# Another written order for the first eleven stretches of a layernorm, attention and gate kernel

## Chip, core and metric

The kernel runs on one core of a Trainium2 chip. The metric is device microseconds of one execution; a time given for a kernel is the median of its runs.

In the text, PE is TensorE (the matmul engine), DVE is VectorE, ACT is ScalarE, POOL is GpSimd and SP is SyncE, which here only issues transfers. PEld is the loading of weights into PE. "SPq" marks the work of SP's queue.

## What is computed

The input x has 2048 rows of 640. Its rows are normalised (mean and variance); the result xn goes through windowed attention with 32 heads of 192 against cached keys and values, whose last 512 positions alone count, and through an output projection. Beside that a small expert layer picks the two rows of xn with the largest score, passes them through a gated feed-forward layer and adds the result to these rows; a silu of that gates the attention.

```python
def _A_ref(x, k_cache, v_cache, wq, wo):
    W = min(4096, max(256, Sk // 4))
    q = (x @ wq).reshape(B, Sq, Hq, Dh) ...
    scores = einsum("bhqd,bhkd->bhqk", q, k) * (Dh ** -0.5)
    p = softmax(scores, axis=-1)
    o = einsum("bhqk,bhkd->bhqd", p, v)
    return o.transpose(...).reshape(B, Sq, Hq * Dh) @ wo

xn = _layernorm(x, axis=-1)
s = _A_ref(xn, A_k_cache, A_v_cache, A_wq, A_wo)
g = _silu(_B_ref(xn, B_w_r, B_w_gate, B_w_up, B_w_down))
return x + s * g
```

All inputs and the output are bf16; W is 512.

## The kernel before

**Tiling.** The 2048 rows are 16 tiles of 128. The 32 heads go in eight groups of four, a group in two pairs of heads. A step is one group, one block of four tiles (t5) and one pair; a unit is one tile of a step, so that unit n belongs to step n // 4 and there are 256 units. A unit's work: scores of both heads (128 x 512 each, two matmuls a head because 192 = 128 + 64), the row maximum, the exponential with its sum, a transpose of the probabilities by DMA, P V (eight matmuls), a division by the sums, a transpose of the output by DMA. Two units of the same tile in the two pairs of a group then give one output projection (W), which is added up in s_acc over the groups.

**Stretches.** The units are put into stretches: units 0 and 1, units 2 and 3, then three at a time (4 to 6, 7 to 9, and so on, line 90); unit 36 is the third of stretch 12. In a stretch the scores of its units come first, then the maxima and exponentials, while PE does query products, P V of the stretch before and output projections.

**Order.** The kernel sets the order of the instructions on every engine itself (line 46). A program text of tokens is walked, and every token appends its instructions to the engines that it uses; each engine and each engine's DMA queue works through its own instructions in that order and waits at each for its operands. The text FIRST (line 853) is written by hand for stretches 0 to 10; from stretch 11 on stretch() (line 823) makes the tokens by a rule. The tokens that matter here:

- `x.t.lo.hi` loads tiles lo to hi of block t of x, on SP's queue, with `.a` on ACT's (load_x, line 98; two blocks have room, so block 2 waits until block 0 has been normalised); `k.p.h` loads the keys of a head of pair p (line 114), `wq.p`, `v.p`, `wo.g.h` the weights and values.
- `bn.n.c` takes the statistics of half a tile on DVE, the second half adds the aggregate (line 162). `as.n` takes a whole tile's on ACT in two passes (line 230), with a small step on POOL. `sq` and `rc` make 1/sqrt of the variance for tiles 0 and 1 on ACT and DVE; `pw.lo.hi` makes it for two to four tiles in four small POOL steps (line 211). `sx` and `ex` have ACT load the Sqrt and the Exp table.
- `ap.n.e` normalises tile n into xn on engine e: `v` DVE, `a` ACT, `g` POOL (line 245).
- `turn.n.e` transposes a tile of xn on PE and copies it out of PSUM on engine e (line 257); `xT.lo.hi` does it by DMA (line 263). `kt.q.e` transposes half the first pair's keys on PE (line 267); `kT.p` does a later pair's by DMA.
- `q.i.c` is a query product: a third c of the pair's queries for all four tiles of step i, five matmuls; with `.lo.hi` for a part of the tiles (line 297). `qe.i.c.e` scales it out of PSUM into qT on engine e (line 307).
- `S.j` scores, `M.n.h` maximum of a head (DVE), `E.n.h` exponential (ACT), `P.n` transpose of the probabilities (SP's queue), `R.j` reciprocals of the sums, `O.n` P V, `Oe.n.e` its eviction with the division, `T.j` transpose of a stretch's outputs (SP's queue), `W.w` output projection, `We.w.e` its eviction.
- `z.1` is a matmul of zeros that nobody reads. `B.j.s` runs what the expert layer has due there; in stretches 0 to 10 nothing is due, so these tokens do nothing.

**PSUM.** Six buffers ("p", one bank each) rotate through scores, projections, the keys' turns and those P V outputs that are written `OO.a.b` or `O.n.g`; two buffers ("f") rotate through query products, the turns of xn and the P V outputs written `O.n` (lines 72 to 79). A buffer is free when its eviction has run.

**The token's engine letter.** first() (line 654) reads it from the last field alone:

```python
op, *n = token.split(".")
e = n[-1] if n and n[-1] in "avgh" else None
n = [int(c) for c in n if c not in "avgh"]
```

scaled() (line 290) uses DVE for "v" and ACT for anything else.

Of the kernel before, what the change touches and what calls it, by code (L numbers as in the profile page):

```python
# [21 lines left out]
def kernel(ctx, tc, A_x, A_k_cache, A_v_cache, A_wq, A_wo, B_x, B_w_r, B_w_gate, B_w_up, B_w_down, out):  # L22
    nc = tc.nc
    P = 128
    _, S, D = A_x.shape
# [88 lines left out]
    def k_load(p, hh, eng):  # L114
        if hh == 0:
            kraw_of[p] = kraw_pool.tile([P, NJ, 2, Dh], BF16, name="k_raw")
        eng.dma_start(out=kraw_of[p][:, :, hh, :], in_=k_win[2 * p + hh].rearrange("(p j) d -> p j d", j=NJ))
# [536 lines left out]
    def first(token):  # L654
        op, *n = token.split(".")
        e = n[-1] if n and n[-1] in "avgh" else None
# [255 lines left out]
```

## Time and profile before

| what | us |
|---|---|
| median of three runs | 797.73 (797.13 to 799.15) |
| profiled execution | 799.47 |
| its span, first to last instruction | 797.7 |
| PE busy | 783.4 (98%) |
| DVE busy | 623.7 (78%) |
| ACT busy | 479.8 (60%) |
| POOL busy | 175.9 (22%) |

A row of a timeline has the start, the length, the engine (ending in q for an issued transfer), the line of the kernel, the operation, what it writes and reads, and how many were merged into it; a bracket at its end has the time that the engine stood idle before it, and what ended that. The length of a merged transfer row is that of its issues on the queue's engine with the waits between. A row of a group has line, engine, operation, what it writes and reads, shapes, count, then busy us and the mean ns of one, then the idle time before them. A row of windows has the window and its length, then the busy us of each engine with its instructions, the granted clock of PE as a share of full speed, the DMA share and GB/s. Matmuls overlap, so the times of single matmul rows can run into each other by a fraction of a microsecond.

### The profile page before, as it was taken

Reading aid. Unit: us, or ns where it says so; the run is one execution under the profiler, and the core shown is the slowest. Engines: PE = TensorE matmul, PEld = TensorE weight load, DVE = VectorE, ACT = ScalarE, POOL = GpSimd, SP = SyncE. Lnnn points to the kernel's source line nnn. Section 1 sums busy time; section 2 is a strip of 40 time slices with the busy share of each in tenths; the row PEclk is TensorE's granted clock in tenths of the full one; section 3 lists DMA queues with packets and bytes.
Section 4 is the critical chain, followed back from the end, with each engine's and each line's share of the span. In section 5 each row is a group of like instructions: output and inputs, shape, how many; then the busy total and the mean of one; then the engine's idle time right before and its main releaser. Section 6 shows DMA issues by size and latency. Waiting matters only on the chain.

```text
span 797.7 us, 15636 instructions
## 1 busy us (share of the span) xinstructions
PE 783.4 (98%) x5751; PEld 482.3 (60%) x5751; DVE 623.7 (78%) x1242; ACT 479.8 (60%) x1291; POOL 175.9 (22%) x193
## 2 busy tenths in 40 slices
PE   7889999999999999999999999999999999999998
PEld 4456556665666665666656666666665666656666
DVE  6976658989787777777787777777788988777786
ACT  5976666555656555665556565556666876565652
POOL 1320000000000000000000499980000000265966
PEclk9999999999999999999999999999999999999999
DMA  8999997799979999799998899979997899997995
GB/s 236 206 213 208 187 197 133 140 183 199 179 123 218 186 209 212 134 216 210 181 215 156 168 180 205 164 121 184 196 184 131 132 186 205 177 199 145 182 165 146
DMA packets 453773, 143.80 MB, mean 180 GB/s; under 512 B 422350, under 2 KB 453328, under 8 KB 453696
## 3 DMA queue, kind: packets, MB, share of 16 engines
q1 hardware_dynamic: 450512, 139.63, 94.4%
q0 software_dynamic: 736, 1.84, 0.8%
q10 hardware_dynamic: 2448, 1.33, 0.6%
q8 instruction: 45, 0.74, 0.4%
q14 instruction: 32, 0.26, 0.1%
HBM read 39.98 MB, written 2.62 MB: 53 GB/s over the span
## 4 chain that ended last, share of the span: by engine, by line
PE 91%; DMA 1%; DVE 0%; ACT 0%; SPq 0%; issue 0%; ACTq 0%
PE w_ps L406 26%; PE q_ps L303 25%; PE o_ps L358 20%; PE sc L317 13%; PE sc L324 8%; DMA kT<-k_raw 1%; PE gu_ps L576 0%; DVE nm L332 0%; ACT pexp L339 0%; PE y_ps L613 0%; DVE fin_o L433 0%; DVE w_ps L431 0%; PE tp_o L391 0%; ACT o_sb L371 0%; SPq L379 0%
## 5 line engine op out<-in xcount | busy, mean ns | idle before, releaser
L339 ACT ACTIVATE pexp<-sc,nm 128x512 bf16<-128x512 f32 x512 | 348.0, 695 | 266.6 <-issue 234.0
L332 DVE TENSOR_REDUCE nm<-sc 128x1 f32<-128x512 f32 x512 | 315.3, 683 | 83.1 <-PE sc L324 83.0
L303 PE MATMUL q_ps<-xnT,wq_p 128*128 128x512 bf16 (+1 forms) x975 | 226.2, 377 | 2.6 <-DVE xnT L261 1.3
L406 PE MATMUL w_ps<-wo_g,oT 128*128 128x320 bf16 x1542 | 222.9, 299 | 0.0
L406 PEld LDWEIGHTS <-oT 128*128 128x128 bf16 x1542 | 150.4, 98 | 70.6
L358 PE MATMUL o_ps<-v_sb,pT 128*128 128x192 bf16 x2048 | 184.6, 246 | 2.7 <-DMA pT<-pexp 1.8
L358 PEld LDWEIGHTS <-pT 128*128 128x128 bf16 x2048 | 171.1, 98 | 16.7 <-DMA pT<-pexp 3.6
L373 DVE TENSOR_TENSOR o_sb<-o_ps,lsum 128x384 bf16<-128x384 f32 x246 | 135.7, 557 | 39.1 <-PE o_ps L358 20.5
L303 PEld LDWEIGHTS <-wq_p 128*128 128x128 bf16 x975 | 88.7, 98 | 125.6 <-issue 35.8
L317 PE MATMUL sc<-kT,qT 128*128 128x512 bf16 x512 | 125.4, 379 | 2.2 <-DMA kT<-k_raw 1.7
L420 DVE TENSOR_TENSOR s_acc<-s_acc,w_ps 128x320 f32<-128x320 f32 x192 | 92.7, 484 | 30.6 <-PE w_ps L406 30.6
L339 ACT ACTIVATION_READ_ACCUMULATOR pexp<-sc,nm 128x1 f32 x512 | 109.5, 214 | 0.0
L295 ACT ACTIVATE qT<-q_ps 128x512 bf16<-128x512 f32 (+1 forms) x180 | 99.5, 606 | 5.0 <-PE q_ps L303 5.0
L317 PEld LDWEIGHTS <-qT 128*128 128x128 bf16 x512 | 48.4, 98 | 44.3 <-DMA kT<-k_raw 2.2
L324 PE MATMUL sc<-kT,qT 64*128 64x512 bf16 x512 | 70.2, 380 | 0.0
L324 PEld LDWEIGHTS <-qT 64*128 64x128 bf16 x512 | 18.1, 94 | 46.8 <-issue 36.5
L650 POOL TENSOR_TENSOR s_acc<-s_acc,xn 128x640 f32<-128x640 f32 x16 | 23.0, 1435 | 102.4 <-DVE s_acc L420 102.3
L629 POOL TENSOR_TENSOR xn<-xn,yh 128x640 bf16<-128x640 bf16 x32 | 44.6, 1394 | 2.7
L619 POOL DMA_DIRECT2D y_d<-y_sb x4 | 2.2, 551 | 181.2 <-DVE y_sb L616 181.2
L496 POOL DMA_DIRECT2D c_d<-cand x1 | 0.5, 544 | 170.7 <-DVE cand L494 170.7
L651 POOL TENSOR_TENSOR s_acc<-s_acc,x_fin 128x640 f32<-128x640 f32 x16 | 22.4, 1398 | 61.4 <-DMA x_fin<-in_A_x_dram 60.5
L628 POOL TENSOR_SCALAR yh<-y_bc,oh 128x640 bf16<-128x640 bf16 x32 | 25.5, 798 | 5.7 <-DMA y_bc<-y_d 4.1
(109 smaller groups left out, 229.2 us busy)
## 6 DMA issues: line engine op xcount, KB each, us to landing
wq_p<-in_A_wq_dram SPq DMA_DIRECT2D x16, 480.0 KB, 5.0
wo_g<-in_A_wo_dram SPq DMA_DIRECT2D x16, 480.0 KB, 4.5
v_sb<-in_A_v_cache_dram SPq DMA_DIRECT2D x16, 384.0 KB, 4.0
k_raw<-in_A_k_cache_dram SPq DMA_DIRECT2D x29, 192.0 KB, 3.3
pT<-pexp SPq DMA_TRANSPOSE x256, 3.6
x_fin<-in_A_x_dram SPq DMA_DIRECT2D x16, 160.0 KB, 2.9
x_in<-in_A_x_dram SPq DMA_DIRECT2D x6, 320.0 KB, 4.0
wgu<-in_B_w_gate_dram SPq DMA_DIRECT2D x15, 128.0 KB, 3.1
```

What stands on the lines that cost most here:

```text
L295: nc.scalar.activation(out=out, in_=in_, func=ACT.Copy, scale=scale)
L303: nc.tensor.matmul(q_ps, lhsT=wq_of[g * PAIRS + pr][:, dc, c * P:(c + 1) * P], rhs=xnT[:, t5 * 4 + lo:t5 * 4 + hi, dc, :], start=(dc == 0) ...
L317: nc.tensor.matmul(sc_of[n][hh], lhsT=qT_of[i][:, 2 * hh, u * P:(u + 1) * P], rhs=kp[:, :, 2 * hh, :], start=True, stop=False)
L324: nc.tensor.matmul(sc_of[n][hh], lhsT=qT_of[i][hs, 1, u * P:(u + 1) * P], rhs=kp[hs, :, 1, :], start=False, stop=True)
L332: nc.vector.tensor_reduce(out=nm_of[j][:, c:c + 1], in_=sc_of[n][hh], axis=AX.X, op=ALU.max, negate=True)
L339: nc.scalar.activation(out=pe_of[n][:, hh, :], in_=sc_of[n][hh], func=ACT.Exp, bias=nm_of[j][:, c:c + 1], scale=1.0, accum_out=l_of[j][:, ...
L358: nc.tensor.matmul(ps[:, hh, :], lhsT=pT_of[n][:, hh, jj, :], rhs=v_sb[:, hh, jj, :], start=(jj == 0), stop=(jj == NJ - 1))
L373: nc.vector.tensor_tensor(out=osb_of[j][:, m], in0=ps, in1=l_of[j][:, 2 * m:2 * m + 2].unsqueeze(2).to_broadcast([P, 2, Dh]), op=ALU.mult)
L406: nc.tensor.matmul(w_ps, lhsT=oT_of[j][:, stretches[j].index(n), c % 3, :], rhs=wo_of[g][:, c, lo:hi], start=(c == 0), stop=(c == CPG - 1))
L420: nc.vector.tensor_tensor(out=acc, in0=acc, in1=w_ps, op=ALU.add)
L628: nc.gpsimd.tensor_scalar(out=yh, in0=M["y_bc"][:, j, :], scalar1=M["oh"][:, n, j:j + 1], scalar2=0.0, op0=ALU.mult, op1=ALU.add)
L629: nc.gpsimd.tensor_tensor(out=xn[:, n, :], in0=xn[:, n, :], in1=yh, op=ALU.add)
```

## The change

The text FIRST is replaced by another order of nearly the same tokens; the work of stretches 0 to 10 is the same, and what follows is untouched.

- Loads: tiles 1 and 2 of x come in one transfer on SP's queue, tile 3 and both heads of the first keys follow there, where tile 3 and the second head were on ACT's queue; block 1 comes tile by tile, tile 4 last; v.1 moves ahead of wq.1; block 2 in three parts. k.1.1 may now stand ahead of k.1.0, so k_load takes the buffer at whichever comes first.
- Ahead of S.0: the Exp table, the turns of tiles 2 and 3, the statistics of tiles 5 and 6 and tile 7's on ACT; the second half of the keys is copied out by DVE and tile 1 by ACT.
- Statistics: eleven tiles on DVE and five on ACT in both, but tiles 5 and 12 change sides with 4 and 7; the order changes.
- Applies: DVE 8 before, 6 after; ACT 2 and 0; POOL 6 and 10.
- The engine letter is now found anywhere in a token, so that the half query products, which all went out on ACT, go where their letter says: three of eight on DVE. The first product of step 2 is now in two halves too.
- P V in the scores' buffers: 16 units before (the `OO` pairs), 12 after, named one by one (`O.n.g`).
- Output projections 0 to 9: evictions on DVE 4 before, 7 after.
- Two transposes of outputs (T.2, T.9) go in two parts. In stretch 10 the transposes of keys 2 and 3 stand in another place of SP's order.
- Six single `z.1` before S.0 where there were three.

The diff, with stretches 6 to 9 left out:

```diff
--- before.py
+++ after.py
@@ -112,7 +112,7 @@
         eng.dma_start(out=wq_of[p][:, lo:hi, :], in_=wq_v[:, lo:hi, p * 3 * P:(p + 1) * 3 * P])

     def k_load(p, hh, eng):
-        if hh == 0:
+        if p not in kraw_of:
             kraw_of[p] = kraw_pool.tile([P, NJ, 2, Dh], BF16, name="k_raw")
         eng.dma_start(out=kraw_of[p][:, :, hh, :], in_=k_win[2 * p + hh].rearrange("(p j) d -> p j d", j=NJ))

@@ -653,7 +653,7 @@

     def first(token):
         op, *n = token.split(".")
-        e = n[-1] if n and n[-1] in "avgh" else None
+        e = next((c for c in n if c in "avgh"), None)
         n = [int(c) for c in n if c not in "avgh"]
         queue = {"a": nc.scalar, "g": nc.gpsimd}.get(e, nc.sync)
         if op == "bn":
@@ -851,18 +851,18 @@

     J0 = 11
     FIRST = """
-x.0.0.1.a x.0.1.2 bn.0.0 x.0.3.4.a bn.0.1 k.0.0 bn.1.0 B.2.0 x.0.2.3 k.0.1.a sq.0.1 wq.0 rc.0.1 sx B.3.3 bn.1.1 ap.0.v x.1.0.2 sq.1.2 rc.1.2 z.1 z.1 z.1 kt.0.a turn.0.a bn.3.0 kt.1.a bn.3.1 ap.1.v turn.1.v bn.2.0 bn.2.1 q.0.0.0.2 x.1.2.4 qe.0.0.v.0.2 q.0.2.0.2 q.0.1.0.2 v.0 qe.0.2.v.0.2 bn.4.0 qe.0.1.v.0.2
-S.0 bn.4.1 pw.2.4 ex bn.6.0 ap.2.v k.1.0 ap.3.v M.0.0 turn.2.a turn.3.v M.0.1 q.0.0.2.4 wq.1 E.0.0 k.1.1 qe.0.0.v.2.4 q.0.2.2.4 bn.7.0 B.3.0 E.0.1 q.0.1.2.4 qe.0.2.v.2.4 x.2.2.4 bn.7.1 qe.0.1.v.2.4 bn.6.1 M.1.0 x.2.0.2 as.5 M.1.1 pw.4.8
-S.1 B.3.1 M.2.0 q.1.2 M.3.0 B.4.0 qe.1.2.v M.2.1 v.1 q.1.1 kT.1 E.1.0 q.1.0 P.0 E.1.1 ap.4.v qe.1.1.a M.3.1 ap.6.v E.2.0 qe.1.0.v B.2.2 E.3.0 R.0 ap.5.g P.1 E.3.1 B.5.3 bn.9.0 O.0 ap.7.g E.2.1 as.8 bn.9.1 bn.11.0 Oe.0.v xT.4.6
-S.2 M.4.0 M.6.0 bn.11.1 M.5.0 as.10 xT.6.8 P.2 E.5.0 O.1 P.3 Oe.1.v E.6.0 M.4.1 pw.8.12 q.2.0 E.4.0 M.5.1 B.3.2 B.5.2 qe.2.0.v q.2.2 x.3.0.2 x.3.2.4 E.4.1 ap.11.v E.5.1 T.0 M.6.1 P.4 qe.2.2.v R.1 q.2.1 qe.2.1.v ap.10.g bn.13.0 E.6.1 P.6
-S.3 R.2 M.7.0 as.12 O.2 E.7.0 M.8.0 Oe.2.v ap.8.a M.7.1 O.3 Oe.3.v E.7.1 P.5 q.3.1 qe.3.1.a M.8.1 E.8.0 ap.9.g M.9.1 B.4.3 E.8.1 xT.10.12 M.9.0 T.1 q.3.0 E.9.0 q.3.2 OO.4.5 qe.3.0.v E.9.1 qe.3.2.v Oe.4.a as.15 R.3 Oe.5.v
-S.4 O.6 xT.8.10 P.8 bn.13.1 M.10.0 P.7 Oe.6.a M.11.0 q.4.1 M.12.0 M.10.1 qe.4.1.v B.2.3 P.9 wo.0.0 E.11.0 bn.14.0 bn.14.1 E.12.0 wo.0.1 M.11.1 E.10.0 T.2 E.10.1 B.7.2 E.11.1 M.12.1 E.12.1 OO.7.8 Oe.7.v O.9 P.11 P.10 P.12 Oe.8.v Oe.9.v
-S.5 q.4.0 pw.12.16 M.14.0 M.13.0 qe.4.0.a ap.15.v R.4 M.13.1 M.15.0 B.2.1 M.14.1 q.5.0 E.13.0 ap.14.g B.6.2 B.6.1 M.15.1 E.13.1 q.4.2 E.14.0 qe.5.0.v W.0 E.14.1 B.10.3 E.15.0 We.0.v OO.10.11 ap.13.g Oe.10.a Oe.11.a qe.4.2.v xT.14.16 E.15.1
...
-S.10 M.28.1 qe.8.1.a M.28.0 E.28.0 M.29.0 q.9.0 B.7.0 kT.2 P.25 M.29.1 O.24 B.8.3 P.26 B.8.2 P.27 M.30.0 E.28.1 R.9 qe.9.0.v Oe.24.a OO.25.26 T.7 E.29.0 E.29.1 M.30.1 B.9.3 T.8 O.27 q.8.2 P.28 Oe.25.a v.3 wo.1.1 E.30.0 W.8 E.30.1 B.10.1 B.9.2 We.8.a Oe.26.v P.30 P.29 Oe.27.a T.9 qe.8.2.a W.9 kT.3 We.9.a
+B.4.0 x.0.0.1.a x.0.1.3 z.1 bn.0.0 x.0.3.4 k.0.0 z.1 bn.1.0 bn.0.1 k.0.1 wq.0 sq.0.1 bn.1.1 z.1 rc.0.1 bn.2.0 z.1 sq.1.2 ap.0.v x.1.1.2 x.1.2.3 rc.1.2 bn.3.0 sx ex ap.1.v x.1.3.4 turn.0.a bn.2.1 bn.3.1 pw.2.4 turn.1.a kt.0.a x.1.0.1 kt.1.v B.5.2 z.1 q.0.2.0.2 qe.0.2.a.0.2 ap.2.g v.0 bn.5.0 ap.3.v B.3.1 q.0.0.0.2 bn.6.0 k.1.1 q.0.1.0.2 qe.0.1.v.0.2 qe.0.0.a.0.2 turn.3.v bn.6.1 z.1 as.7 k.1.0 turn.2.v bn.5.1 v.1
+S.0 M.0.0 wq.1 q.0.0.2.4 M.0.1 q.0.2.2.4 as.4 qe.0.0.a.2.4 q.0.1.2.4 qe.0.2.v.2.4 pw.4.8 x.2.0.1 ap.4.g E.0.0 ap.7.g M.1.0 ap.5.v E.0.1 M.1.1 qe.0.1.a.2.4 x.2.1.3 x.2.3.4 E.1.0
+S.1 q.1.2 kT.1 q.1.0 E.1.1 M.3.0 M.2.1 P.0 M.3.1 ap.6.g xT.4.6 M.2.0 E.3.0 P.1 qe.1.2.a qe.1.0.v E.3.1 q.1.1 O.0 E.2.0 E.2.1 bn.9.0 qe.1.1.v B.3.3
+S.2 bn.11.0 O.1 R.0 xT.6.8 P.3 R.1 bn.11.1 Oe.0.v M.4.1 M.4.0 as.8 P.2 B.7.0 x.3.2.4 q.2.0.0.2 as.10 Oe.1.v qe.2.0.a.0.2 B.2.2 q.2.0.2.4 B.2.0 x.3.0.2 M.6.0 E.4.0 bn.9.1 E.6.0 q.2.2 E.4.1 M.5.0 T.0 E.5.0 qe.2.0.v.2.4 B.10.2 B.3.0 q.2.1 M.5.1 E.5.1 M.6.1 pw.8.12 qe.2.2.v E.6.1 ap.9.g qe.2.1.v B.5.3 ap.10.v bn.14.0 P.4
+S.3 O.2 P.5 O.3 as.15 M.7.0 M.8.0 ap.8.g Oe.2.a M.9.1 Oe.3.v E.7.0 P.6 bn.13.0 xT.8.10 ap.11.v q.3.0 E.8.0 q.3.1 M.7.1 M.8.1 qe.3.0.a E.7.1 qe.3.1.v B.2.3 xT.10.12 q.3.2 E.8.1 O.4 M.9.0 P.7 O.5.g R.2 qe.3.2.a T.1 B.10.0 bn.13.1 Oe.4.v Oe.5.v B.4.1 E.9.0 E.9.1 P.9 bn.12.0 bn.12.1
+S.4 O.6 M.10.0 M.12.0 M.10.1 q.4.1 P.8 wo.0.0 E.10.0 R.3 B.4.3 Oe.6.v O.7.g q.4.0 M.11.0 qe.4.1.v O.9 E.10.1 M.12.1 E.11.0 M.11.1 E.12.0 E.12.1 wo.0.1 O.8.g Oe.7.v Oe.8.v E.11.1 B.2.1 P.10
+S.5 bn.14.1 qe.4.0.a Oe.9.a T.2.0.1 M.13.0 M.13.1 M.14.0 M.15.0 E.13.0 q.5.0 q.4.2 T.2.1.3 R.4 P.11 M.15.1 B.10.3 E.14.0 E.13.1 M.14.1 P.12 pw.12.16 ap.15.g O.10.g ap.14.g qe.5.0.v ap.13.g Oe.10.a qe.4.2.v W.0 E.15.0 We.0.v B.6.2 P.13 E.14.1 B.8.2 P.14 ap.12.g B.6.1 O.11.g xT.14.16 E.15.1 Oe.11.v B.7.1 O.12 Oe.12.v
...
+S.10 M.28.0 M.28.1 O.24 M.30.0 E.28.0 P.27 q.8.2 Oe.24.v B.7.2 E.28.1 E.30.0 M.30.1 R.9 qe.8.2.v kT.2 T.7 B.8.1 O.27.g M.29.0 T.8 E.29.0 O.25.g E.30.1 O.26.g q.9.0 M.29.1 E.29.1 kT.3 Oe.25.v W.8 Oe.26.a Oe.27.a P.28 wo.1.0 P.30 We.8.v W.9 We.9.a P.29 wo.1.1 v.3 qe.9.0.v T.9.0.2 T.9.2.3 B.9.2
     """.split()

     for token in FIRST:
```

8 lines of the change are left out of this document (4 added, 4 removed).

## The prediction

> **What bounds the kernel now.** I read the page's slices first, then a table of windows cut at starts of score matmuls, then TensorE's (PE's) own timeline for its gaps, then the DMA queue. The page:
>
> ```profile
> span 797.7 us, 15636 instructions
> ...
> PE   7889999999999999999999999999999999999998
> ```
>
> PE is full everywhere but at the two ends. The change touches only the first end, so the table of windows divides that (busy us of PE, weight loads, VectorE, ScalarE and GpSimd, then granted clock, DMA share, GB/s):
>
> ```profile
> 13.12:24.34 11.22, 9.71 (x66) 4.83 (x64) 10.37 (x24) 10.31 (x27) 4.27 (x9) 1.00 0.92 186
> 24.34:34.33 9.99, 8.68 (x49) 3.42 (x48) 9.44 (x21) 9.59 (x25) 3.31 (x9) 1.00 1.12 217
> 34.33:50.31 15.98, 14.22 (x110) 8.59 (x109) 13.74 (x28) 13.09 (x36) 4.31 (x9) 1.00 1.05 201
> ...
> 59.46:106.53 47.07, 47.07 (x347) 29.79 (x346) 29.36 (x55) 32.42 (x90) 0.00 (x0) 1.00 1.04 193
> 106.53:120.00 13.47, 11.74 (x79) 6.16 (x77) 8.17 (x16) 6.95 (x20) 0.00 (x0) 1.00 1.19 213
> 120.00:780.00 660.00, 660.00 (x4882) 408.32 (x4881) 527.64 (x1041) 393.60 (x1066) 148.86 (x139) 1.00 0.96 176
> ```
>
> From 59.46 to 106.53 and from 120 to 780 us PE never rests. There the time is the sum of its matmuls, which the change leaves alone, so what is won or lost before 120 us reaches the end one for one. Before 50 us VectorE is as full as PE: 10.37 of 11.22 us, 9.44 of 9.99, 13.74 of 15.98. In that part its written order decides when PE gets its operands. What can be won is PE's idle time; its timeline names the gaps, in brackets:
>
> ```profile
> 14.61 0.73 PE L260 MATMUL tp<-ident,xn 128*128 128x128 bf16 x10
> 15.93 1.90 PE L303 MATMUL q_ps<-xnT,wq_p 128*128 128x256 bf16 x15 [0.58 <-DVE xnT L261]
> ...
> 23.67 0.83 PE L358 MATMUL o_ps<-v_sb,pT 128*128 128x192 bf16 x8 [0.90 <-ACT pexp L339]
> ...
> 28.23 2.32 PE L303 MATMUL q_ps<-xnT,wq_p 128*128 128x512 bf16 x10 [0.91 <-DVE mv L167]
> 30.95 1.24 PE L303 MATMUL q_ps<-xnT,wq_p 128*128 128x512 bf16 x5 [0.40 <-DVE qT L293]
> ...
> 46.18 2.15 PE L358 MATMUL o_ps<-v_sb,pT 128*128 128x192 bf16 x24 [1.76 <-DMA pT<-pexp]
> ...
> 57.73 0.38 PE L317 MATMUL sc<-kT,qT 128*128 128x512 bf16 x1 [0.19 <-ACT o_sb L371]
> 58.39 0.38 PE L317 MATMUL sc<-kT,qT 128*128 128x512 bf16 x1 [0.29 <-ACT pexp L339]
> ...
> 117.21 0.61 PE L317 MATMUL sc<-kT,qT 128*128 128x512 bf16 x2 [1.73 <-DMA kT<-k_raw]
> ```
>
> From the first scores (S.0, 13.12 us) to stretch 11 (S.11, 106.53) PE is idle 0.58 + 0.90 + 0.91 + 0.40 + 1.76 + 0.19 + 0.29 = 5.03 us, and 1.73 us more inside the scores of stretch 12: 6.76 in all.
>
> **The change, part by part.** Rows for durations: VectorE (14.4 to 41.2 us), two forms of other engines (0 to 110 us), and steps of PE's chain, which give 1.08 for a query product, 0.66 for P V of a unit and 1.29 + 0.75 = 2.04 for the scores of three units:
>
> ```profile
> L332 DVE TENSOR_REDUCE nm<-sc 128x1 f32<-128x512 f32 x20 | 13.0, 678 | 1.0 <-PE sc L324 0.9
> L293 DVE TENSOR_SCALAR qT<-q_ps 128x512 bf16<-128x512 f32 x7 | 4.8, 680 | 0.2
> L165 DVE BATCH_NORM_STATS2 stats<-x_in 128x6 f32<-128x320 bf16 x9 | 4.1, 469 | 0.0
> L373 DVE TENSOR_TENSOR o_sb<-o_ps,lsum 128x384 bf16<-128x384 f32 x5 | 2.7, 550 | 0.0
> L253 DVE TENSOR_SCALAR xn<-x_in,mv,rstd 128x640 bf16<-128x640 bf16 x3 | 1.6, 547 | 0.0
> L167 DVE BATCH_NORM_AGGREGATE mv<-stats 128x2 f32<-128x12 f32 x4 | 0.8, 208 | 0.1
> L261 DVE COPY xnT<-tp 128x640 bf16<-128x640 bf16 x1 | 0.5, 491 | 0.2 <-PE tp L260 0.2
> ```
>
> ```profile
> L251 POOL TENSOR_SCALAR xn<-x_in,rstd,nmr 128x640 bf16<-128x640 bf16 x6 | 5.5, 918 | 0.4
> ...
> L295 ACT ACTIVATE qT<-q_ps 128x256 bf16<-128x256 f32 x6 | 2.2, 385 | 1.9 <-PE q_ps L303 1.9
> ```
>
> ```profile
> 60.29 1.08 PE q_ps L303 x5
> ...
> 68.17 0.66 PE o_ps L358 x8
> ...
> 96.31 1.29 PE sc L317 x6
> 97.61 0.75 PE sc L324 x6
> ```
>
> *Up to the first scores.* Today VectorE stands idle until tile 1 and the keys are through PE:
>
> ```profile
> 10.45 0.49 DVE L261 COPY xnT<-tp 128x640 bf16<-128x640 bf16 x1 [2.29 <-PE tp L260]
> ```
>
> The new order brings tiles 1 and 2 in one transfer and the keys behind tile 3 on SyncE's queue, takes the statistics of tiles 0 to 3 in one run, loads the Exp table before the turns instead of behind S.0, and turns tiles 2 and 3 ahead of S.0. By the rows: eight halves, four aggregates and two applies are 8 x 0.469 + 4 x 0.208 + 2 x 0.547 = 5.7 us from about 4.0 us; two tile copies, a key copy, tile 3's apply, three more halves with an aggregate and a scaled half query are about 4.2 more, with some 0.9 of waiting for the key transposes among them, and PE's last five transposes come with the last copy but one. I put S.0 at 13.4 us, 0.3 later than now. But the ten transposes of 0.73 us that follow S.0 today are done by then, and the gap of 0.58 behind them goes. The keys in one queue I cost at nothing: their turn on PE stands behind both tiles' turns; if that cover went, a key landing 1 us later would put S.0 1 us back. Tile 2's apply on GpSimd (0.918, behind four small steps for tiles 2 and 3) is hidden by three half queries on PE; uncovered, it would cost those 0.9.
>
> *From S.0 to the scores of stretch 3 (13.1 to 34.3 us).* VectorE is the limit, so I count its work up to the last scaled query of step 2. The statistics of tiles 4 and 7 leave, tile 5's enter: -(2 x 0.469 + 0.208) = -1.15. Applies: seven now, four then: -3 x 0.547 = -1.64. Scaled queries: five whole ones now, then four whole and three halves. The letters in the half-query tokens had no effect so far (the parser looked at the last field alone), and all six halves ran on ScalarE, 0.385 each; now three run on VectorE. No row has that form: at least half of 0.680, at most all of it; I take 0.38, since ScalarE's half costs that. So 3 x 0.38 - 0.68 = +0.46 (0.34 to 1.36). The second copy of the first keys comes over from ScalarE: 768 columns, by the 640-column copy's 0.491, +0.59 (0.49 to twice that). Sum -1.74. The 2.29 of idle above shrinks to the 0.9 I left: -1.4. Together -3.1, of which VectorE may lose all to new waits, or nothing. New waits stand where PSUM's two f buffers are freed by VectorE steps written behind row maxima (Oe.1.v behind M.4.1 and M.4.0; qe.2.0.v.2.4 behind M.6.0, bn.9.1 and M.5.0), with the next query product queued behind each on PE. I take 0.6 for them, less than one maximum: **-2.5 us** at the end of S.3 (0 to -3.4).
>
> Four more applies go to GpSimd, beside VectorE's own:
>
> ```profile
> 30.81 0.76 DVE L253 TENSOR_SCALAR xn<-x_in,mv,rstd 128x640 bf16<-128x640 bf16 x1
> ```
>
> This apply ran beside one of GpSimd's and took 0.76 where the mean, it included, is 0.547. One such loss is inside the 0.6. [...]
>
> *The DMA queue in the same part.* Rows of SyncE's queue, then the times from issue to landing of the key transposes:
>
> ```profile
> 14.05 0.89 SPq L101 DMA_DIRECT2D x_in<-in_A_x_dram  x2
> ...
> 15.56 2.00 SPq L121 DMA_TRANSPOSE kT<-k_raw  x1
> ...
> 40.54 4.96 SPq L344 DMA_TRANSPOSE pT<-pexp  x3
> ...
> 98.18 4.53 SPq L379 DMA_TRANSPOSE oT<-o_sb  x2
> ...
> 111.55 1.51 SPq L121 DMA_TRANSPOSE kT<-k_raw  x1
> ```
>
> ```profile
> DMA to landing us min/median/max: 3.8/5.6/7.2
> ```
>
> Pair 1's keys were issued at 15.56 and landed 7.2 us later, at 22.8; P V of unit 0 started at 23.67, its probabilities 0.9 behind the keys in the same queue. The third group of x, which held that queue until 14.05 for tile 3's apply, is let go with tile 2's, some 1.5 us earlier, and so is all behind it: keys near 21.2, unit 0 near 22.1. PE asks at 13.4 + 1.36 (scores of two units) + 1.90 (three half products) + 1.36 + 3.24 (three products) = 21.3. So of the 0.90 gap little is left; this lets PE follow VectorE and is not counted again. Uncovered, it would be the 0.9.
>
> *Stretches 3 to 5 (34.3 to 50.3).* Two applies (1.1) and some 0.1 of statistics that used to come earlier fall here: +1.2 for VectorE. The 1.76 gap was PE at P V of unit 7, whose probabilities went second in the 40.54 row; now unit 7 goes first and alone ahead of T.1. O.4 takes an f buffer that qe.3.1.v frees behind M.7.1 and M.8.1; I take 0.4. Net -1.76 + 1.2 + 0.4: **-0.2** (-1.76 to +1.6).
>
> *Stretches 5 and 6.* The 0.19 and 0.29 came from ScalarE, late in freeing score banks. Both its applies leave for GpSimd: **-0.3** (0 to -0.48). Step 2's first product in two halves costs five more weight loads and matmuls: 1.90 / 15 x 10 - 1.08 = +0.2, half of it in the wait before: **+0.1**.
>
> *Stretch 10.* The new order of the queue: P.27, kT.2, T.7, T.8, kT.3, and then P.28 to P.30, V and the turned outputs. Today kT.3 is last, issued at 111.55, and the scores of unit 36 start at 117.21. Six places earlier it lands long before: **-1.7** (0 if something holds it, V's wait among what it now passes). But T.7 comes behind kT.2, and W.8 needs T.7. PE reaches W.8 2.04 + 0.66 + 1.08 + 3 x 0.66 + 1.08 = 6.8 us into the stretch. Today T.7 goes out at 98.18, 1.9 after that stretch's first scores (96.31). Then kT.2 goes out there, lands 3.8 to 5.6 us later if no loads are ahead of it, and T.7 some 0.9 behind it: at 6.6 to 8.4. A wait of 0 to 1.6; near the lower end, since no load is ahead: **+0.4**.
>
> *The clock.*
>
> ```profile
> 9.00:10.00 1.00, 1.00 (x13) 0.50 1.08 373
> ...
> 12.00:13.00 1.00, 1.00 (x10) 1.00 1.08 297
> ```
>
> The granted clock was 0.50 from 9 to 10 us and full from 12 on. In the new order PE's work before 13 us is as thin, with single warm-up products between, so a half-clock stretch will fall somewhere in it; the difference I cost at nothing, bounds -0.7 (the transposes and halves it slowed) and +1.6 (half of the 3.2 us of S.0 and the half products after it). [...]
>
> **Sum:** -2.5 - 0.2 - 0.3 + 0.1 - 1.7 + 0.4 = -4.2 us. The profiled execution took 799.47 us around its span of 797.7; the runs shown have the median 797.73, 1.7 less. The terms are differences, so I take them off the median: 793.5.
>
> **Rivals.**
> *Only the late keys are mended.* VectorE has the statistics of eleven tiles and the same maxima in both orders and is over 85% busy until 50 us; every gap taken away comes back as another wait on it. Then only the 1.73 in stretch 12 goes: 796.0. For it speak the three windows, against it the 2.29 of idle.
> *The change doesn't do what it says.* As before, but the key transposes moved forward in stretch 10 only exchange waits: W.8 stands for T.7's bound of 1.6, -1.73 + 1.6: 797.6. For it the queue's order, against it the landings of 3.8.
> *Slower: PE held at the two f buffers.* Query products and f-bank P V outputs rotate through two buffers; now only 0.40 (30.95 row) of the gaps is of that kind. In the new order seven steps of PE between stretch 2 and stretch 5 (second half of q.2.0, q.2.1, S.3, q.3.1, O.4, q.4.0, O.9) need an eviction that VectorE reaches behind maxima. Two maxima (1.36) for each are 9.5 us, while the 5.03 and the 1.73 go, and 0.3 and 0.4 come for S.0 and W.8: +3.4, 801.1. It decides as soon as PE's idle time from S.0 to S.11 passes 5.03 + 1.73 - 0.7 = 6.1 us. Against it: ScalarE takes every second eviction there.
>
> **How the numbers follow.** Forecast 0.58, only the keys 0.14, no change 0.08, slower 0.20. What a measurement of this kernel can tell from no change is about 0.3%, 2.4 us; the two middle cases lie inside that. So faster 0.58, same 0.22, slower 0.20. The forecast's own range is 790.5 (all 6.76 of gaps and 0.4 of the start gone) to 795.3. With the middle cases, and up to where the slower one begins, 790.5 to 799.9.
>
> **What would show it.** Right: S.0 near 13.4 us, scores of stretch 3 ending near 32 instead of 34.3, no VectorE gap over 1 us between 5 and 30 us, less than 4 us of PE idle from S.0 to S.11, no gap ahead of unit 36. Wrong: S.0 past 15 us; PE gaps released by scaled queries or P V evictions (L293, L295, L373) of over 4 us in sum; a gap over 1 us at W.8 released by T.7; VectorE's half evictions as long as whole ones.

## The result, and the profile after

The median went from 797.91 us (795.48 to 801.85, 20 runs) to 795.46 us (794.17 to 797.81, 20 runs): a ratio of 0.9965, 95% interval 0.9952 to 0.9977, so 2.4 us less, a little over what a measurement of this kernel can tell from no change. The profiled execution of the new kernel took 796.88 us around a span of 795.1.

The page of the new kernel, its head and the slices of PE and of PE's clock:

```profile
span 795.1 us, 15675 instructions
...
PE   8999999999999999999999999999999999999998
...
PEclk9999999999999999999999999999999999999999
```

The windows of the new kernel, cut at about the same work as before (first scores, stretch 2, end of the scores of stretch 3, then unit 7's stretch; below the dots stretch 6 to the end of stretch 10, then 11 and most of 12, and the rest):

```profile
12.20:22.25 10.05, 9.03 (x57) 4.36 (x55) 9.76 (x23) 9.90 (x28) 4.53 (x9) 1.00 1.18 240
22.25:31.32 9.07, 8.63 (x54) 3.94 (x53) 7.93 (x18) 7.81 (x22) 2.78 (x8) 1.00 1.10 204
31.32:47.29 15.97, 14.92 (x111) 8.86 (x111) 14.37 (x31) 12.36 (x33) 1.02 (x2) 1.00 1.09 193
...
55.50:102.92 47.42, 47.42 (x345) 29.53 (x344) 30.60 (x59) 31.98 (x89) 0.00 (x0) 1.00 1.11 199
102.92:115.00 12.08, 12.08 (x82) 6.50 (x80) 8.67 (x16) 6.97 (x19) 0.00 (x0) 1.00 1.13 203
115.00:780.00 665.00, 663.21 (x4904) 410.07 (x4903) 529.44 (x1046) 394.59 (x1066) 150.26 (x140) 1.00 0.96 177
```

The first two windows are 10.05 and 9.07 us long where they were 11.22 and 9.99. In the window around stretch 12 PE is now busy for all of its 12.08 us. But in the long last window PE is busy for 663.21 of 665.00 us, where it never rested before. PE's timeline names the idle time that is left:

```profile
12.20 1.03 PE L317 MATMUL sc<-kT,qT 128*128 128x512 bf16 x4
...
21.58 0.83 PE L358 MATMUL o_ps<-v_sb,pT 128*128 128x192 bf16 x8 [0.99 <-DMA pT<-pexp]
...
28.00 1.24 PE L303 MATMUL q_ps<-xnT,wq_p 128*128 128x512 bf16 x5 [0.34 <-DVE qT L293]
29.08 1.56 PE L317 MATMUL sc<-kT,qT 128*128 128x512 bf16 x6
...
32.97 1.24 PE L303 MATMUL q_ps<-xnT,wq_p 128*128 128x512 bf16 x5 [0.16 <-ACT o_sb L371]
...
43.99 0.83 PE L358 MATMUL o_ps<-v_sb,pT 128*128 128x192 bf16 x8 [0.48 <-DMA pT<-pexp]
45.21 0.83 PE L358 MATMUL o_ps<-v_sb,pT 128*128 128x192 bf16 x8 [0.39 <-DMA pT<-pexp]
...
53.96 0.83 PE L358 MATMUL o_ps<-v_sb,pT 128*128 128x192 bf16 x8 [0.41 <-DMA pT<-pexp]
...
195.92 1.25 PE L303 MATMUL q_ps<-xnT,wq_p 128*128 128x512 bf16 x5 [1.37 <-DMA wq_p<-in_A_wq_dram]
199.03 1.24 PE L303 MATMUL q_ps<-xnT,wq_p 128*128 128x512 bf16 x5 [0.23 <-ACT qT L295]
```

From S.0 to S.11 the gaps are 0.99 + 0.34 + 0.16 + 0.48 + 0.39 + 0.41 = 2.77 us (5.03 before); the gap of 1.73 before unit 36 is gone; nothing waits at W.8. A wait that was not there before stands at 195.92: the second query product of stretch 21, for the weights of pair 5. VectorE has one gap of over 1 us between 5 and 30 us, at the first maximum of stretch 2, whose scores come behind the gap of 0.99 on PE:

```profile
24.07 1.29 DVE L332 TENSOR_REDUCE nm<-sc 128x1 f32<-128x512 f32 x2 [1.07 <-PE sc L324]
```

To see where each microsecond goes, the table takes the start of each stretch's scores (the first L317 row of the stretch in PE's timeline), new minus old. The first pair of profiles is the one shown so far. The second pair is from two runs of the unchanged kernels side by side on one chip, told below as experiments; there the gaps from S.0 to S.11 are 3.03 us (new) and 5.15 (old).

| up to | predicted, sum so far | first pair | second pair |
|---|---|---|---|
| S.0 | +0.3 | -0.92 | +0.22 |
| S.3 | -2.5 | -2.95 | -1.79 |
| S.11 | -2.9 | -3.60 | -2.47 |
| S.13 | -4.2 | -5.51 | -3.78 |
| S.22 | -4.2 | -3.26 | -2.33 |
| span | -4.2 | -2.6 | -1.6 |

S.85 is the last stretch. In both pairs more is won by stretch 13 than arrives at the end.

### The profile page after: what moved, and what is told of

Its sections match the earlier page's. It is cut to its first block, busy times and chain, and to the rows that moved or that the text cites. A ratio compares the mean times of both kernels' runs of the same rounds, so it can differ in the third digit from the quotient of the medians.

```text
span 795.1 us, 15675 instructions
## 1 busy us (share of the span) xinstructions
PE 783.9 (99%) x5759; PEld 481.9 (61%) x5759; DVE 624.1 (78%) x1247; ACT 477.0 (60%) x1285; POOL 179.1 (23%) x197
## 4 chain that ended last, share of the span: by engine, by line
PE 74%; DMA 1%; ACT 0%; DVE 0%; issue 0%; ACTq 0%
PE w_ps L406 21%; PE q_ps L303 20%; PE o_ps L358 16%; PE sc L317 10%; PE sc L324 6%; DMA pT<-pexp 1%; PE gu_ps L576 0%; ACT pexp L339 0%; PE y_ps L613 0%; DVE fin_o L433 0%; DVE w_ps L431 0%; PE tp_o L391 0%; ACT qT L295 0%; ACTq L339 0%
## 5 line engine op out<-in xcount | busy, mean ns | idle before, releaser
L317 PE MATMUL sc<-kT,qT 128*128 128x512 bf16 x512 | 125.1, 379 | 0.1
L317 PEld LDWEIGHTS <-qT 128*128 128x128 bf16 x512 | 48.5, 98 | 41.8 <-issue 1.2
```

The lines of the kernel that those rows point to most:

```text
L317: nc.tensor.matmul(sc_of[n][hh], lhsT=qT_of[i][:, 2 * hh, u * P:(u + 1) * P], rhs=kp[:, :, 2 * hh, :], start=True, stop=False)
```

## Experiments

Where a median is given, the old kernel's beside it was taken on the same chip in the same job. In a diff of the order the tokens are broken into short lines; the order is split at white space, so that changes nothing.

### The two kernels again

*New kernel, unchanged.* 

> The new kernel unchanged, profiled once more. Theory (the stand of the transfers at stretch 20 and the wait for the weights of pair 5 at 195.9 us belong to that one execution): no gap over 0.5 us at that query product, and 5 us ahead of the old kernel's trace from stretch 13 on. Rival (the new order always has these weights late): the same gap of 1 to 1.9 us again.

Measured: 795.63 us (795.33 to 795.99, 8 runs) beside 797.91, ratio 0.996 [0.9946, 0.9974].

*Old kernel, unchanged, a single run.* 

> The old kernel unchanged, profiled once more. Theory (the profiled execution of the old kernel, 799.47 us, lies 1.6 us above the median because one or two of its gaps are not in most executions): the gap of 1.73 us ahead of unit 36, or the 1.76 before P V of unit 7, is smaller by 1 us or more. Rival (the gaps are there in every execution, and the excess of the profiled one comes from elsewhere): both within 0.3 us of the first trace.

Measured: 797.57 us, span 795.7. Rows of PE's timeline, first the old kernel's:

```profile
11.74 1.03 PE L317 MATMUL sc<-kT,qT 128*128 128x512 bf16 x4
...
44.74 2.15 PE L358 MATMUL o_ps<-v_sb,pT 128*128 128x192 bf16 x24 [1.63 <-DMA pT<-pexp]
...
115.22 0.60 PE L317 MATMUL sc<-kT,qT 128*128 128x512 bf16 x2 [1.13 <-DMA kT<-k_raw]
```

then the new one's:

```profile
11.96 1.03 PE L317 MATMUL sc<-kT,qT 128*128 128x512 bf16 x4
...
194.90 1.25 PE L303 MATMUL q_ps<-xnT,wq_p 128*128 128x512 bf16 x5 [0.62 <-DMA wq_p<-in_A_wq_dram]
...
197.98 1.24 PE L303 MATMUL q_ps<-xnT,wq_p 128*128 128x512 bf16 x5 [0.19 <-ACT qT L295]
```

The gap before unit 36 was 1.13 us this time and the one before unit 7 1.63, and S.0 came at 11.74 us instead of 13.12. So the first profile of the old kernel lay some 2 us above this one (span 797.7 against 795.7), most of it in its first 13 us. Neither expectation of the old kernel holds as written: one gap is 0.60 us smaller, not 1, and the other nearly the same. The wait for the weights of pair 5 came again in the new kernel with half the length, 0.62 us, which lies between what its two expectations said.

### The clock

Windows of PE's recorded clock, first the old kernel (first profile): the one before the clock fell, the one at half clock, and the one with the wait before unit 36, behind which the clock did not fall:

```profile
4.92:8.34 3.42, 1.34 (x10) 0.60 (x9) 3.11 (x11) 0.68 (x3) 0.00 (x0) 1.00 0.98 311
8.34:11.75 3.41, 2.73 (x25) 2.31 (x23) 1.28 (x3) 2.10 (x3) 0.00 (x0) 0.50 1.11 331
114.17:117.58 3.41, 1.68 (x12) 0.69 (x9) 0.94 (x2) 0.00 (x0) 0.00 (x0) 1.00 1.28 127
```

then the new kernel, with the windows counted from its own first full clock:

```profile
5.09:8.50 3.41, 2.23 (x21) 1.21 (x20) 3.31 (x13) 2.37 (x6) 0.00 (x0) 1.00 1.08 328
8.50:11.92 3.42, 3.15 (x32) 2.40 (x30) 2.88 (x9) 3.16 (x7) 2.17 (x5) 1.00 1.12 334
```

PE was busy for 1.34 of 3.42 us before the old kernel's clock fell to half; in the new one the thinnest of its start has 2.23. The full clock's end and return were recorded 3.413 us apart. To see what holds the clock up, the matmuls of zeros were taken out of the new kernel:

```diff
-z.1
 ...
```

(all six single `z.1` before S.0; nothing that the output needs; the ten at the very start, line 140, stay). 

> The new kernel without the six single warm-up products. Theory: TensorE's clock stays full in the new start only because of them; without them it is halved for some 3.4 us somewhere between 8 and 14 us, the scores of stretch 0 start about 1 us later (13.2 instead of 12.2) and the median is 0.5 to 1 us over the new kernel's. Rival: the turns and half products alone keep the clock up, and nothing changes (0.3 us).

Measured: 795.02 us (794.25 to 795.82, 6 runs), ratio 0.9953 [0.9935, 0.9971]. In its profile the clock was first recorded as full at 13.28 us instead of 5.09 (the fifteen half query products at 9.59 us took 3.41 us, in the new kernel's first profile 1.88), and S.0 started at 13.79, 1.8 later than in the second profile of the new kernel:

```profile
13.79 1.03 PE L317 MATMUL sc<-kT,qT 128*128 128x512 bf16 x4
```

By S.2 0.64 of that was left, but from S.6 to S.13 it was 1.41 again. At S.22 the two are level (0.02), because no wait for the weights of pair 5 came in this profile. So in the profiles the matmuls of zeros win 1.8 us up to S.0 and 1.4 up to S.13, and none of it is there at S.22; in the median they win nothing, and the theory's 0.5 to 1 us did not come.

Each run lists its mean granted clock, and one half-clock window of 3.4 us takes 0.002 off it; the half clock behind PE's last work takes some 0.001 at most, and the time ahead of the first full clock is not counted (the profile just told lists 1.000). With the new start and its zeros 1 of 66 runs had 0.998 or less (the new kernel, the weights earlier, the new order up to stretch 1, the turned tiles and the keys on two queues, told below), without them 4 of 6 here and 8 of 10 in the version meant to beat both. So the zeros do hold the clock up; that this saves time is not shown, since the medians of these two are 795.02 and 795.88.

Of the 75 runs of the old kernel made beside these experiments 36 had 0.998 or less, median 800.0 us; the other 39 had 797.3. All 28 runs of the new kernel (20 and 8) had 0.999 or more, median 795.5. Beside the old kernel's runs at full clock the new order is thus 1.8 us shorter; the rest of the 2.4, some 0.6, goes with the falls of the old kernel's clock. Whether the fall or what came ahead of it costs the time is open: the waits that thin out a window cost time of their own.

### The halves of the change

*New order up to stretch 1, old order from stretch 2.* The tokens that the new order has left over by then go to the start of S.2:

```diff
 S.2
+R.0 Oe.0.v bn.9.1 bn.11.0 as.8
 M.4.0 M.6.0 bn.11.1 M.5.0
 ...
```

> The new order up to the end of stretch 1, the old one from stretch 2 on (five tokens that the old order had done by then are put at the start of stretch 2). Theory: the scores of stretch 2 start at 22.3 us as in the new kernel, 2 us ahead; about 1.5 of that is kept, since VectorE has the five tokens still to do, and the gaps of 1.76 before P V of unit 7 and of 1.73 before unit 36 stay: 796 to 797. Rival: VectorE is full until 50 us in the old order too, so all of it is given back by stretch 5 and the median is the old 797.9.

Measured: 796.87 us (796.19 to 800.07, 12 runs) beside 798.37, ratio 0.9987 [0.9971, 1.0003].

*Old order up to stretch 1, new order from stretch 2*, without the five tokens that are done by then:

```diff
 S.2
-bn.11.0
 O.1
-R.0
 ...
```

> The other half: the old order up to the end of stretch 1, the new one from stretch 2 on (the five tokens that are done by then left out there). Theory (gains add by place): scores of stretch 2 start at 24.3 us as in the old kernel, the gaps before P V of unit 7 and ahead of unit 36 are gone, 2 to 3 us less than the old kernel: 795 to 796. Rival (only the start counts): within 0.5 us of the old kernel.

Measured: 796.98 us (796.32 to 800.29, 12 runs) beside 797.91, ratio 0.9989 [0.9975, 1.0003].

Neither half's interval excludes no change; their medians are 1.5 and 0.9 us below the old kernel's, which add up to the whole's 2.4. So each half seems to have a part, and neither is shown alone. In the profile of the first half the wait before unit 36 is still there with 1.00 us; in that of the second it is gone. 4 of 12 runs with the old start had a clock of 0.998 or less, 1 of 12 with the new one.

### The keys of pair 3

*In the old order, moved forward.*

```diff
-T.8 O.27 q.8.2
+T.8 kT.3 O.27 q.8.2
 ...
-W.9 kT.3 We.9.a
+W.9 We.9.a
```

> The old kernel with the transposed keys of pair 3 put right behind T.8 in stretch 10 instead of last. Theory (each gap of TensorE before 120 us is worth its length): 1.73 us less than the old kernel, ratio 0.998, and no gap ahead of unit 36. Rival: what stands behind the keys in the queue (P.28, P.30, P.29, V of pair 3, T.9) comes late in their place, and nothing is won.

Measured: 797.63 us (796.46 to 801.02) beside 798.37, ratio 0.9998 [0.9979, 1.0016]. In its profile the gap before unit 36 is gone, 1.91 us between S.12 and S.13, and from there to S.85 only 0.11 us is lost. But this execution began an extra microsecond late:

```profile
9.14 0.56 PE L275 MATMUL tp_k<-ident,k_raw 128*128 128x128 bf16 x5 [2.59 <-DMA k_raw<-in_A_k_cache_dram]
```

The keys of pair 0, which this edit does not touch, landed at 9.14 instead of 8.14 us, and the clock fell to half at 9.36. The landing at the start differs between executions by as much as the edit is worth; the median leaves it open.

*In the new order, moved back to the end.*

```diff
-E.29.1 kT.3 Oe.25.v
+E.29.1 Oe.25.v
 ...
-T.9.0.2 T.9.2.3 B.9.2
+T.9.0.2 T.9.2.3 kT.3 B.9.2
```

> The new kernel with the transposed keys of pair 3 put last in stretch 10, as in the old one. Theory: 1.5 to 2 us slower than the new kernel (about 797.3), with the gap ahead of unit 36 back. Rival: since stretch 10 starts earlier and the wait is for a transfer, the gap is the same but the new kernel's later loss at the weights of pair 5 shrinks by as much, and the median stays at 795.5.

Measured: 798.98 us (795.8 to 802.09) beside 798.37, ratio 1.0001 [0.9986, 1.0015]. PE's timeline and the windows around the change of the clock in this kernel:

```profile
116.00 1.04 PE L317 MATMUL sc<-kT,qT 128*128 128x512 bf16 x2 [3.03 <-DMA kT<-k_raw]
```

```profile
111.57:114.98 3.41, 1.40 (x11) 0.66 (x8) 1.03 (x2) 0.09 (x1) 0.00 (x0) 1.00 1.53 160
114.98:121.81 6.83, 5.81 (x17) 1.67 (x18) 3.68 (x6) 3.27 (x9) 0.00 (x0) 0.50 0.82 162
```

The wait is 3.03 us, longer than the old kernel's 1.73, and from 114.98 us on the clock is at half for 6.83 us. Between S.12 and S.13 4.06 us are lost against the old kernel's first profile. It is the slowest of the 12 runs; 7 of them had a mean clock of 0.998 or less. Left out of the new order, this one move costs the whole gain in the median. The wait is longer because PE comes to S.12 2.51 us earlier than in the old kernel's first profile, but the keys land only 1.21 earlier (116.00 against 117.21).

### The weights of pair 5

```diff
-        at(n0 - 5, 0, lambda p0=p0: wq_load(p0 + 1, nc.sync))
+        at(n0 - 8, 0, lambda p0=p0: wq_load(p0 + 1, nc.sync))
```

Three units are one stretch earlier. 

> The new kernel with one line changed: from group 2 on the query weights of a group's second pair are loaded one stretch earlier (due 8 units ahead of the group instead of 5). Theory: in the profiled run of the new kernel 5.2 us had been won by stretch 21 and 1.9 of them were lost there, on a query product that waited for these weights; if that loss is usual, this kernel takes about 1.5 to 2 us less than the new one (793.5 to 794) and its trace has no gap at that product. Rival: the wait was an accident of that one execution (a 3 us standstill of the transfers beside an instruction fetch); then the median stays at the new kernel's, 795.5, within 0.5.

Measured: 795.4 us (794.51 to 796.62, 12 runs) beside 798.37, ratio 0.9958 [0.9943, 0.9973]. In its profile, its fastest run, the wait is gone and S.22 starts 3.3 us earlier than in the first profile of the new kernel (6.56 against 3.26 below the old one). But 1.59 of these 3.3 were there at S.13, ahead of anything the edit touches, and stretches 20 and 21 take 0.54 us more than in the first profile of the old kernel, 52 and 53 0.79 more. The median is the new kernel's, as the rival had it: taking this wait away is not shown to win anything. What the other runs lose instead no trace shows.

Why the wait came is seen in the queue. SP's rows of the new kernel, then of the old, and with each the bytes moved, over the 21 us that end 5.85 us (new) and 5.65 us (old) after S.21 starts, with the time from issue to landing of both weights:

```profile
179.39 0.86 SPq L133 DMA_DIRECT2D wo_g<-in_A_wo_dram  x1
180.35 7.39 SPq L344 DMA_TRANSPOSE pT<-pexp  x3
...
190.54 0.62 SPq L112 DMA_DIRECT2D wq_p<-in_A_wq_dram  x1
```

```profile
GB/s 21 0 105 214 200 100 194 183 218 157 119 241 324 330 93 9 10 20 24 80 285 290 227 210 170 211 208 154 150 230 284 114 135 274 334 276 104 144 283 281
...
wo_g<-in_A_wo_dram SPq DMA_DIRECT2D x1, 480.0 KB, 7.3
wq_p<-in_A_wq_dram SPq DMA_DIRECT2D x1, 480.0 KB, 5.3
```

```profile
184.20 0.82 SPq L133 DMA_DIRECT2D wo_g<-in_A_wo_dram  x1
185.12 5.78 SPq L344 DMA_TRANSPOSE pT<-pexp  x3
...
193.76 0.62 SPq L112 DMA_DIRECT2D wq_p<-in_A_wq_dram  x1
```

```profile
GB/s 78 0 25 216 201 195 214 217 211 159 178 239 336 247 179 304 98 8 10 257 290 280 240 205 86 198 249 296 154 322 369 268 190 285 289 223 207 192 215 198
...
wo_g<-in_A_wo_dram SPq DMA_DIRECT2D x1, 480.0 KB, 4.6
wq_p<-in_A_wq_dram SPq DMA_DIRECT2D x1, 480.0 KB, 4.5
```

Each slice is 0.525 us. In the old kernel the transfers stand nearly still (8, 10 GB/s) for two slices, behind the landing of wo_g (184.20 + 4.6), in the new one (9, 10, 20, 24) for four, in the middle of wo_g. So wo_g lands after 7.3 us instead of 4.6, the transposes behind it take 7.39 instead of 5.78, and wq_p leaves 0.61 us before S.21's start (191.15), where it left 2.59 before it (196.35). That is the wait. The standstills lie beside a transfer of the queue of instructions (189.29 us in the old kernel, 183.31 in the new); this is taken up again under the hardware.

In the twelve profiles in which these weights have their old place the loss in stretch 21 goes with the time at which they leave. In eight they leave 1.91 to 3.10 us before S.21, and stretch 21 takes 9.00 to 9.25 us. In four (both of the new kernel, all P V in the f buffers, the turned tiles) they leave 0.61 to 1.41 us before it, and it takes 9.68 to 10.94. PE's lead alone does not bring it. The version with the first keys on two queues is 0.59 us ahead of the new kernel's first profile at S.20; its weights leave 2.87 before S.21 (190.56), and nothing waits:

```profile
187.69 0.62 SPq L112 DMA_DIRECT2D wq_p<-in_A_wq_dram  x1
```

### P V in the scores' banks

All twelve `O.n.g` of the new order written `O.n`, so that every P V goes through the two f buffers:

```diff
-O.5.g
+O.5
 ...
```

> The new kernel with all twelve P V outputs that it writes into a bank of the scores put into the two f buffers instead; everything else stays. Theory (a P V in an f buffer queues behind the eviction of a query product, so the banks of the scores are what lets TensorE run on): new waits by L293 or L373 of 0.2 to 0.5 us at half or more of the twelve places, 2 to 4 us over the new kernel's 795.5, so 797.5 to 799.5. Rival (the evictions are in time anyway, since ScalarE takes every second one): no new gap of over 0.3 us, 795 to 796.

Measured: 807.11 us (805.01 to 807.6, 4 runs) beside 799.19, ratio 1.0097 [1.0066, 1.0127]: 7.9 above the old kernel on its chip and 11.6 above the new kernel's median, three to six times what the theory said. Three of its four runs had a clock of 0.998 or less; the profiled one, the fastest, did not. Some of its gaps in PE's timeline:

```profile
52.93 0.82 PE L358 MATMUL o_ps<-v_sb,pT 128*128 128x192 bf16 x8 [1.73 <-DVE qT L293]
...
74.24 0.82 PE L358 MATMUL o_ps<-v_sb,pT 128*128 128x192 bf16 x8 [2.60 <-ACT qT L295]
...
94.58 0.82 PE L358 MATMUL o_ps<-v_sb,pT 128*128 128x192 bf16 x8 [1.07 <-DVE qT L293]
...
108.31 1.24 PE L303 MATMUL q_ps<-xnT,wq_p 128*128 128x512 bf16 x5 [0.94 <-ACT o_sb L371]
```

Its starts are level with the new kernel's up to S.4 (-0.31) and 9.72 us behind at S.13. Of its 11.05 us of gaps between S.0 and S.11 7.34 end with a scaled query, on either engine, and 3.17 with a P V eviction. The theory had the mechanism and a third of its size.

### The turns of tiles 2 and 3

```diff
-turn.3.v
 bn.6.1 z.1 as.7 k.1.0
-turn.2.v
 bn.5.1 v.1
 S.0 M.0.0
+turn.3.v turn.2.v
 wq.1
 ...
```

> The new kernel with the turns of tiles 2 and 3 written behind the first scores and the first maximum, as in the old order; everything else stays. Theory: the first scores start up to 0.7 us earlier and the half products behind them wait again for the copies, 0.5 to 0.6 us and more since the copies now stand behind a maximum; from stretch 2 on VectorE's work is the same, so what is left there is within 0.6 us, and the time is 795.5 to 796.1. Rival (VectorE's work alone sets the pace, the place of two copies does not matter): starts from stretch 2 on within 0.2 us of the new kernel's, 795.5.

Measured: 795.86 us (795.16 to 797.15, 9 runs) beside 799.19, ratio 0.9947 [0.993, 0.9965]. In PE's timeline:

```profile
14.59 1.88 PE L303 MATMUL q_ps<-xnT,wq_p 128*128 128x256 bf16 x15 [0.82 <-DVE xnT L261]
```

S.0 starts 0.67 us earlier than in the first profile of the new kernel, the gap behind it is back with 0.82, S.1 is 0.77 later, and S.3 starts at the same 29.08 us. Up to there the rival holds in the main (S.2 is 0.39 earlier, where it allowed 0.2): VectorE's work sets the pace, and the place of two copies is worth nothing at S.3. By S.6 the kernel is 0.64 us behind the new one again, at waits of P V for transposed probabilities, so from there on neither expectation fits as written.

### The first keys on two queues

```diff
-x.0.3.4 k.0.0
+x.0.3.4.a k.0.0
 ...
-k.0.1 wq.0
+k.0.1.a wq.0
```

> The new kernel with tile 3 of x and the second head of the first keys on ScalarE's queue again; everything else stays. Theory (as costed in the prediction, nothing: the turn of the keys stands behind both tiles' turns): start of the first scores within 0.3 us of the 11.96 and 12.20 us of the two profiles of the new kernel, 795.5. Rival (the keys' landing decides): the first scores move by the change of the landing, by about 1 us either way, and the time moves by what is left of that at stretch 13.

Measured: 794.37 us (794.05 to 794.92, 5 runs) beside 799.19, ratio 0.9937 [0.9911, 0.9964]. S.0 starts at 12.35 us, within 0.15 of the first profile and 0.39 of the second: the queue of the first keys is worth about nothing at S.0, as costed (the theory allowed 0.3). Its profile shows no wait for pair 5's weights (S.22 2.52 us ahead of the new kernel's first profile), which nothing in the edit asks for. It is the lowest median of all kernels run, but its interval overlaps the new kernel's, and the two were not run on one chip.

### A version meant to beat both

The new kernel without its six `z.1` and with the weights one stretch earlier (the expectation's "three stretches" should read three units). 

> The new kernel without its six matmuls of zeros and with the second weights of each group loaded three stretches earlier. Theory (the two edits each took the wait for the weights of pair 5 away; without it the profiles of either end 1 to 2 us ahead of the new kernel's): 794.0 to 794.8. Rival (each edit only moves the wait to another of the later weights): 795.0 to 795.6, no better than the new kernel.

Measured: 795.88 us (794.58 to 797.04, 10 runs) beside 799.19, ratio 0.9956 [0.994, 0.9973]: no better. Its profile, its fastest run, has no gap from stretch 6 to 780 us and a span of 792.8, but the start is thin:

```profile
5.32:8.73 3.41, 1.29 (x17) 0.90 (x17) 3.31 (x13) 2.41 (x6) 0.00 (x0) 1.00 1.04 317
8.73:12.15 3.42, 3.29 (x22) 2.40 (x19) 2.25 (x6) 2.13 (x5) 2.19 (x5) 0.50 1.11 329
```

8 of its 10 runs have a mean clock of 0.998 or less, and they are no longer than the other two (795.78 and 796.53). No version was shown to beat the new kernel.

## Why the prediction was right, and where it was not

The sign, the mechanism and most of the places were right; the time was forecast as 793.5 and is 795.5. Measured by the second pair, whose two executions both kept the full clock, it holds up to stretch 13 (-3.78 against -4.2) and fails behind it. The 795.5 lies 0.2 above the upper end of the forecast's own range (790.5 to 795.3), inside the whole range, and nearer to the 796.0 of the rival with the late keys only than to 793.5. So the median does not decide between these two. The starts do: at S.11, ahead of these keys, the new order leads by 3.60 and 2.47 us, where that rival had nothing. Of the signs, the end of the scores of stretch 3 (31.32), the idle time of PE up to S.11 (2.77) and the missing gap before unit 36 came as said, S.0 and the gaps of VectorE did not.

- *S.0 at 13.4.* It came at 12.20 and 11.96. The step counted tile 6's second half, its aggregate and a last copy ahead of S.0; VectorE does them at 12.19 and later, and PE does not wait for them. An apply took 0.435 us in the mean, not 0.547, and from 5 us to S.0 VectorE waited 0.51 us (0.16 + 0.35), not 0.9.
- *-2.5 to stretch 3.* -2.95 and -1.79 for S.3. VectorE is the limit there, as the turned tiles show (S.3 unmoved at 29.08 us). The half evictions took 0.42 us (taken: 0.38), the copy of the keys 0.56 (0.59). The gap on VectorE of 1.07 us at 24.07, where none over 1 was to be, follows the gap of 0.99 on PE at P V of unit 0, which I let shrink to little: its probabilities still land late. In the first profile of the new kernel none of VectorE's six applies (0.43 to 0.45 us each) ran beside one of GpSimd's, so the one such loss inside the 0.6 was not put to the test: that the 0.76 us of the one apply in the old profile came from GpSimd is not shown.
- *-0.2, -0.3 and +0.1 to stretch 6.* S.3 to S.11 gave -0.65 and -0.68 against -0.4. The 1.76 at unit 7 became 0.48 and 0.39; the two gaps by ScalarE are gone.
- *-1.7 for the keys of pair 3, +0.4 at W.8.* From S.11 to S.13 the pairs give -1.91 and -1.31 against -1.3. The gap before unit 36 is gone, 1.73 in the first profile and 1.13 in the second; W.8 did not wait at all. Moved back, the keys cost more than the term: the wait was 3.03 us where the old kernel's was 1.73, with PE 2.51 us earlier, and in the profile the clock fell in it, at 114.98 us.
- *The clock at nothing: wrong.* "A half-clock stretch will fall somewhere in it" did not happen in 28 runs. The old kernel's clock fell in nearly half of its runs (36 of 75), and some 0.6 of the 2.4 us between the medians goes with this.
- *"What is won or lost before 120 us reaches the end one for one": this is the step that failed.* PE indeed never rested from 120 to 780 us in the old trace, but the transfers there have their own times. In stretch 13 0.31 us went in both pairs, why stays open. Between S.21 and S.22 1.94 us (first pair) and 1.15 (second) went to the weights of pair 5, held up by a long standstill of the transfers. A lead need not be lost so: in the profile with the old start and the new order from stretch 2 on, 3.67 us ahead of the old kernel's first profile at S.13, all but 0.12 arrives at S.85. And with the weights earlier the wait is gone but the median is no better, so what a usual run loses behind S.13 is known only in part. Behind the last scores another 0.6 went: from the start of S.85 to the end it is 23.53 us in both profiles of the old kernel and 24.08 and 24.14 in those of the new, half of it in a P V of stretch 85 (two units take 1.78 us instead of 1.49) and half behind PE's last matmul. Why that is so stays open.
- *The base.* The gaps were read from an execution that, as the second profile shows, lay about 2 us above a usual one, and were taken off the median. The 1.73 was 1.13 in the other one.

The rival with the two f buffers is a real mechanism: with twelve more P V outputs let into them the kernel is 7.9 us over the old one. This is not the rival's own case, which had seven steps of the new order as it stands and 3.4 us. In the new kernel only 0.34 us of the gaps up to S.11 end with a scaled query, because these twelve are in the scores' banks. That ScalarE takes every second eviction, the prediction's reason against it, would not have been enough: the gap of 2.60 is released by ScalarE.

## What to carry to other kernels

A gain ahead of a stretch in which the bounding engine never rests need not arrive at its end, since the transfers in that stretch have their own times: here 5.51 us at S.13 were 2.6 at the end (first pair), and the keys of pair 3, put last, were waited for 3.03 us instead of 1.73 when PE came 2.51 us earlier. See for each load that is waited for how long before its use it leaves and lands, and see it in more than one profile: the weights of pair 5 left 0.61 to 3.10 us before S.21. Before gaps are added up from one profile, see in the listed clocks and times of the runs whether it is a usual one. A buffer pool of two behind two different evictions is worth checking by moving everything into it: the price of what an order avoids, here 11.6 us between the medians, does not show in its own trace.

## What the runs showed of the hardware

**The clock fell to half behind thin steps.** In the old kernel's first profile the full clock is recorded for 3.413 us (4.92 to 8.34), then the half clock for as long (8.34 to 11.75). Counted in steps of this length from the moment at which PE's clock was first full, the share of PE's busy time in the step just before a fall was 1.34 / 3.42 = 0.39 (old), 0.38 (the version meant to beat both), 0.24 (old order with the keys forward) and 0.41 (keys last in the new order). No step with 0.49 or more, in any of the fourteen profiles up to 780 us, was followed by a fall, the old kernel's at 114.17 us (1.68 of 3.41) among them. That the clock goes by such steps is inferred from these falls, which came at the end of one; whether a limit lies between 0.41 and 0.49, and whether the share alone decides, no run shows.

**Transfers stood still beside fetches of instructions.** The page of the new kernel counts 45 transfers of the larger of its two instruction queues, one in some 18 us:

```profile
q8 instruction: 45, 0.74, 0.4%
```

In its first profile packets of other transfers take 1.3 us or more within 1.5 us of 30 of the 45, mostly up to 2.0 and at 183.3 us 3.0, and at 7 places away from them. That a fetch causes the standstill is inferred from the two lying together; no run took a fetch away. Why one lasted twice as long as most others is open. It came at 0.1 us into stretch 20 in both profiles of the new kernel (3.0 and 2.4 us, both with the wait behind it). Of the twelve profiles with the weights in their old place the four whose stretch 21 is long have packets of 1.9 to 3.0 us there, the eight others of 1.5 to 2.0.

**The start differed by a microsecond.** The first keys landed at 8.14, 9.14, 7.99 and 8.05 us in the four profiles in which the old order issues them at the same place.
